# Half-height score pairs, scanned states and a third seven-product batch in a fused retention and Fourier-mix kernel

## The chip, the cores and the metric

The kernel runs on one core of a Trainium2 chip. The metric is the device time of one execution in microseconds; lower is better. Engines are named as in the profile: PE (TensorE, with PEld for its weight loads), DVE (VectorE), ACT (ScalarE), POOL (GpSimd), SP (SyncE, which issues most of the DMAs).

## The reference

Two stages follow each other. The first is a retention recurrence over q, k, v of 4 batches, 8 heads, 768 steps, 64 channels; the second a Fourier mix with a two-layer network on 4 x 768 rows of 512 channels.

```python
gamma = 1.0 - 2.0 ** (-5.0 - np.arange(H))
for t in range(S):
    state = gamma[None, :, None, None] * state + np.einsum('bhd,bhe->bhde', k[:, :, t], v[:, :, t])
    y[:, :, t] = scale * np.einsum('bhd,bhde->bhe', q[:, :, t], state)
...
X = np.fft.fft(np.fft.fft(x, axis=1), axis=2)
u = x + np.real(X)
un = (u - mu) / np.sqrt(var + 1e-06)
out = u + np.maximum(un @ w_ch1, 0.0) @ w_ch2
```

Here x is y with the heads side by side (4 x 768 x 512), w_ch1 is 512 x 2048, w_ch2 2048 x 512.

## The kernel before, in words

**Retention.** The sequence is cut into six chunks of 128 steps. Heads go in pairs: a pair's 2 x 64 channels fill 128 partitions. Within a chunk, scores are keys times queries (`wkA`, in PSUM), multiplied by a causal mask with the head's decay (`atm`, in SBUF), and then multiplied with the values; across chunks, a 64 x 64 state per head is carried (`wkK` in PSUM, `s16` in SBUF) and multiplied with the queries. Both products add up in `wkY`, which ACT scales and writes as x.

The first batch and the other three differ in how they do that. The first batch keeps both heads' queries in one tile of 128 partitions and multiplies each head's 64 partitions apart: `am_unit` (L563) makes twelve matmuls of 64 x 128 with 128 columns, alternating between the two heads, `kv0_unit` (L591) ten of 64 columns for the states, and one DVE scan (`sc_unit`, L600) carries the states of both heads over all chunks with the decay table `gk5`. Batches two to four pad the queries with zeros, so that each head has a full tile of 128 partitions with the other head's half empty (`q16z`, `qTz`, padded by `pad_unit` and `qt_zeros`): `a_unit` (L689) makes six matmuls of 256 columns in three parts, each followed by one DVE multiply with the ready mask table `maskp` (L691); `kv_unit` (L708) makes five of 128 columns that compute both heads' states and the cross terms too, carried chunk by chunk by one ACT copy (L713) and four DVE steps (L715); `y_unit` handles one head (L729, L732). Keys and queries are transposed by PE in batch two (`t_unit`, L655; the keys of its last two pairs by DMA) and by DMA in batches three and four (`td_unit`).

**Fourier mix and network.** The transforms are matmuls with cosine and sine tables after folds on DVE (`fold_s`, `fold_d`, `fold_e`; `s1_unit`, L861; `s2_unit`, L1015). POOL adds x (`add_x_unit`, L1048 and L1050), DVE and ACT normalize, and the rows are transposed (`unT_unit`). The first layer is `h0_unit` and `h_unit` (L1118, L1105) with the ReLU on ACT or DVE, the second `ch_unit` (L1140), which works with 512 columns, and `rows_out` (L1130). That is so in the first two batches. In batches three and four the second layer is computed in three groups of 256 rows with seven block products instead of eight: `hp_unit` is the first layer (L1193), `sum_unit` the sums on DVE (`j`, L1211), `p_unit` the products (`p`, L1242) and `add_unit` the adding and the output (`q`, L1256). The differences of weight blocks that these need are made once on DVE by `wsum_unit` (`w`, L1181) and lie in the memory of the input tiles `wide` and of two used tables.

**Order.** It is written out by hand. `FIRST` is the first batch, `LATER` the rest; each name is a unit (kind, batch, index, and after @ the engine for its ReLU or copy). `held` keeps each engine's instructions in written order, so a unit that waits holds up all behind it on that engine. `ps_g` has five PSUM buffers for attention and transforms, `ps_pm` three for the network. Inputs come in two sets of tiles: seven buffers `inp` and the four of `wide`.

Of the kernel before, what the change touches and what calls it, by code (L numbers as in the profile page):

```python
# [11 lines left out]
AF = mybir.ActivationFunctionType  # L12
ALU = mybir.AluOpType
# [6 lines left out]
P = 128  # L20
B, H, S, D = 4, 8, 768, 64
DM = 512
# [30 lines left out]
i02 U01@v i03 x03 X03 U02@a x04 X04 i10 i13 i11 l10 x05 X05 i12 cq10 c0010 n04 i22 l11 c0011  # L53
c0012 n05 TB Z u04 i21 c0013 u05 U05@a r00 n03 c0000 c0001 l12 l13 ck10 t10 cv10 i23 ck11 pz01
c0002 s100 s101 c0003 cq11 O00 a101 cq12 u03 O01 cv11 i20 U03@a a100 t11 c0020 a102 ck12 U04@v
cv12 c0021 s110 c0022 s111 y100 y101 h015@v t12 pz00 a111 cq13 a110 h013@a lq20 a112 s120 h011@a
s121 h01B@v h012@v ck13 cv13 s130 s131 y110 y111 t13 lk20 lv20 lq21 c0023 a120 a122 h01E@a
h010@a a121 a132 ck20 h018@a a131 y121 y120 O02 pz10 a130 h014@a lk21 lv21 h01C@a h016@a y131
fs10 lq22 lk22 lv22 y130 fs11 fd10 r01 h01D@a fd11 h01A@a tk20 h017@a h019@a c0100 c0101 cq20
h01F@a c0102 c0103 g10 fe10 fe11 f100@v f101@v gr11@v f110@v f111@a tq20 gr13@a cq21 gr10@v O03  # L60
c0110 g112 x11 x10 X11 n11 x12 c0120 X10 n10 X12 n12 c0111 lq23 c0112 c0121 pz11 cv20 gr12@a u11
c0113 O04 u10 ck22 u12 c0122 c0123 U10@v U11@a U12@v tq21 a200 ck21 cv22 O05 x13 tk21 X13 s200
s201 cq22 x14 X14 h107@a h103@a h108@a cv21 x15 h10C@a h10B@a h106@v h102@a a202 lk23 h104@v
a201 h105@a h100@a n14 lv23 cq23 h101@a y200 y201 tk22 h10A@v tq22 h10D@a lq30 X15 h10E@a n13
a210 u13 h10F@a ck23 tk23 a212 s210 s211 a211 cv23 n15 U13@d u14 U14@d w10 r10 c1020 c1000
h109@a a222 a220 c1001 y210 y211 tq23 c1002 s230 s231 a221 w11 c1010 c1011 c1012 u15 U15@d s220
c1003 O10 c1013 s221 c1021 w21 lk30 lv30 lq31 r11 a231 y220 a232 y221 h110@a lk31 lv31 fs20 a230
c1022 O11 c1023 O12 y230 h11E@a fd20 y231 fs21 h11D@a fd21 cq30 h119@a h11A@a g20 ck31 h117@a
h113@a fe21 h11F@a tq30 h112@a h115@a f211@a fe20 ck30 f210@v w20 f200@v gr20@v f201@a h111@v
gr21@v gr23@v lq32 lk32 h11C@a h116@v tk31 tk30 gr22@a g212 lv32 x21 cq31 x20 h114@a X21 h11B@v  # L70
tq31 n21 cv31 c1110 X20 x23 X23 c1120 h118@a x22 cv30 s310 x25 u21 n20 lq33 u20 U21@d X22 c1121
cq32 w41 c1100 n23 n22 cv32 x24 c1111 c1101 c1112 U20@d ck32 c1102 c1103 O13 X24 a301 lk33 a302
u22 c1113 O14 c1122 a312 w40 c1123 U22@d a311 X25 O15 n25 H202@s s300 ck33 s301 H204@s H203@a
u23 a300 s311 H201@a a310 H200@a j20104 H207@a j20178 y300 w31 H205@s y301 w30 tk32 j20204
j20404 cq33 H206@s j20147 j20347 r20 j20378 y310 U23@d tk33 j20278 y311 p201 p204 lv33 cv33 tq32
q201 j20247 j20304 j20447 tq33 p202 q202 p206 p205 q206 p207 u25 n24 q205 u24 j20478 q207 s320
s330 r21 s321 H217@a j21178 a320 p203 q203 j21278 U24@d a322 a321 a331 H213@s H210@s s331 j21478
H212@a H211@a j21104 j21304 j21204 j21378 a332 H215@a H214@s j21404 H216@a a330 y321 j21147
j21347 p211 j21247 q211 j21447 y320 fs30 y331 y330 p214 p216 fs31 q216 fd31 p215 q215 U25@d p217
g30 fd30 fe30 fe31 p212 p213 q212 f300@a f301@a q217 f310@v f311@a q213 H221@a g312 x31 gr30@v  # L80
X31 x30 X30 n31 n30 H226@a H222@s H223@a H220@a j22104 j22204 u31 x32 H224@b H225@s H227@b r22
j22404 p221 q221 j22147 j22178 gr31@a X32 j22247 u30 gr33@a p224 p225 j22278 j22304 p226 p222
U31@d j22447 U30@d j22378 q225 gr32@a j22347 j22478 q226 n32 u32 q222 p223 q223 p227 q227 x33
H300@s x35 H304@a r30 H302@v H303@b H301@a j30104 X33 H306@s H305@s n33 U32@d j30204 j30404
j30304 H307@b j30148 X35 j30248 j30448 x34 p301 q301 p304 p305 p302 q305 p306 j30348 q306 u33
U33@d q302 p303 q303 n35 p307 q307 X34 H317@v n34 H314@a u34 U34@d H312@v H315@a H313@a H311@b
H310@s H316@s j31104 j31204 j31148 j31248 j31348 j31304 r31 j31404 p311 q311 p314 p315 q315
j31448 p312 p316 q316 q312 u35 U35@d p313 q313 p317 q317 H321@a H320@a H322@a j32103 j32303
H327@b H326@a j32168 H324@a H323@s j32203 H325@s j32403 j32368 j32136 j32236 r32 j32436 p321
p322 j32336 p324 p325 q321 j32268 p326 q322 q325 j32468 p323 q326 p327 q323 q327  # L90
# [7 lines left out]
def kernel(  # L98
# [13 lines left out]
    def pool(name, bufs, **kw):  # L112
# [6 lines left out]
    tp = pool("tp", 2)  # L119
    ap_ = pool("ap", 2)  # L120
# [8 lines left out]
    obp = pool("obp", 2)  # L129
# [15 lines left out]
    maskp = const.tile([P, NHP, 2, P], f32, tag="maskp")  # L145
# [3 lines left out]
    gk5 = const.tile([P, 2, D, NCH - 1], f32, tag="gk5")  # L149
    t2 = gk5[:, 0].rearrange("p e c -> p (e c)").bitcast(f16)[:, 0:520].rearrange(  # L150
        "p (n w) -> p n w", n=4)
# [58 lines left out]
    def filler32(n):  # L210
        def run():
            for _ in range(n):
# [7 lines left out]
    turns = early + [x for b in (1, 2) for i in range(4) for x in [(n, b, i) for n in "qkv"]  # L220
                     if x not in early]
# [81 lines left out]
    nc.gpsimd.memset(gk5[:, :, :, 0:1], 0.0)  # L303
# [6 lines left out]
    def gk_unit(i, eng):  # L310
        copy = nc.scalar.copy if eng == "a" else nc.gpsimd.tensor_copy
        hp = ORD0[i]
        return lambda: copy(gk5[:, i % 2, :, 1:], gk2[:, hp:hp + 1].unsqueeze(1).to_broadcast(
            [P, D, NCH - 2]))

    def late_consts():
        with tc.issue_after(lb[0]["una"].ins):
            for h in range(H):
                nc.scalar.activation(maskp[:, h // 2, h % 2], maskf, AF.Copy, bias=0.0,
                                     scale=float(gam[h] ** (-P)))  # L320
# [16 lines left out]

    def pad_unit(j, h):
        return lambda: nc.vector.memset(qzs[j][:, h, :, D - D * h:P - D * h], 0.0)

    def qt_zeros():
        for j in range(2):
            nc.vector.memset(qts[j][0:D, 1], 0.0)
            nc.vector.memset(qts[j][D:P, 0], 0.0)
# [88 lines left out]
    for j in range(2):  # L433
        x = const.tile([P, NCH, 2, XW], f16, tag=f"x16_{j}", name=f"x16_{j}")
        xts.append(x)
        qz = const.tile([P, 2, NCH, P], f16, tag=f"q16z_{j}", name=f"q16z_{j}")
        qzs.append(qz)
        qt = const.tile([P, 2, NCH, P], f16, tag=f"qTz_{j}", name=f"qTz_{j}")
# [16 lines left out]
    def cq_unit(b, i):  # L455
        def run():
            q16, q32 = qzs[i % 2], in_of.pop(("q", b, i))
            if b < NPE:
                q16 = q16_of[b, i] = q16.rearrange("p h c d -> p (h c d)")[
                    :, 0:NCH * P].rearrange("p (c h d) -> p c h d", c=NCH, h=2)  # L460
                nc.gpsimd.tensor_scalar(out=q16, in0=q32.rearrange("p h c d -> p c h d"),
                                        scalar1=1.0, scalar2=1.0, op0=ALU.mult, op1=ALU.mult)
                return
            for h2 in range(2):
                dst = q16[:, h2, :, D * h2:D * h2 + D]
                nc.gpsimd.tensor_scalar(out=dst, in0=q32[:, h2], scalar1=1.0, scalar2=1.0,
                                        op0=ALU.mult, op1=ALU.mult)
            q16_of[b, i] = q16
        return run
# [20 lines left out]
    def q0_unit(i):  # L490
        def run():
            q16 = q16_of[0, i] = qzs[i % 2].rearrange("p h c d -> p (h c d)")[
                :, 0:NCH * P].rearrange("p (c h d) -> p c h d", c=NCH, h=2)
# [34 lines left out]
    def t0_unit(i, part):  # L528
        def run():
            if part == 0:  # L530
                at[0, i] = dict(kT=tp.tile([P, NCH, P], f16, tag="kT", name="kT"),
                                qT=qts[i % 2][:, 0])
# [62 lines left out]
    def sc_unit(i):  # L595
        def run():
            st = at[0, i]
            st["s16"] = sp.tile([P, D, NCH - 1], f16, tag="s16", name="s16",
                                padded_shape=[P, P, NCH - 1])
            nc.vector.tensor_tensor_scan(  # L600
                out=st["s16"].rearrange("p e c -> p (e c)"),
                data0=gk5[:, i % 2].rearrange("p e c -> p (e c)"),
# [41 lines left out]
    def t_unit(b, i):  # L644
        def run():
# [3 lines left out]
            for dst, src in ((qT, q16_of[b, i]), (kT, kd_of[b, i])):  # L649
# [7 lines left out]
                if dst is qT:  # L657
                    for h2 in range(2):
                        rows = slice(D * h2, D * h2 + D)
                        nc.scalar.copy(  # L660
                            qT[rows, h2].rearrange("p c t -> p (c t)").rearrange(
# [771 lines left out]
```

## Time and profile before

| | before |
|---|---|
| median of 3 runs | 237.56 us (237.46 to 237.72) |
| profiled execution | 237.73 us |
| its span in the profile | 235.7 us |
| busy: PE, DVE, ACT, POOL | 223.2, 197.0, 133.3, 83.6 us |
| first matmul of the network | 32.8 us |
| last DVE instruction starts | 231.74 us |
| TensorE clock granted | full in all slices |

Busy times are shares of the span by engine; they overlap. A row of the timeline or of the chain has start, length and work; a row of groups has line, engine, operation, output and inputs, count, busy us, mean ns of one, and the engine's idle time before them.

### The profile page before, as it was taken

To read this page: it belongs to the slowest core of one execution; us is meant where nothing else is said; L and a number is where in the kernel's file an instruction comes from. 1 tells how busy PE (TensorE), PEld (TensorE's weight loads), DVE (VectorE), ACT (ScalarE), POOL (GpSimd) and SP (SyncE) were. 2 spreads that over 40 slices of the span, in tenths; PEclk is the share of its full clock that TensorE was granted. 3 is DMA by queue.
4 is the path that set the end of the run, shared out by engine and by line. 5 is a ranking of instruction groups with operands and counts; after the bars stand their busy time and mean duration, and the time that the engine had idled before them with its cause. 6 is when DMAs were issued, how large, how long until landed. Compare 5 with 4: busy or idle time off the path is not lost.

```text
span 235.7 us, 5892 instructions
## 1 busy us (share of the span) xinstructions
PE 223.2 (95%) x2271; PEld 168.9 (72%) x2271; DVE 197.0 (84%) x490; ACT 133.3 (57%) x304; POOL 83.6 (35%) x148
## 2 busy tenths in 40 slices
PE   0898999999999999999999999999989999999993
PEld 0366769767765747665667548998979899888882
DVE  8789986978898989797998899889998987949373
ACT  5989758486687258554286435834617846062530
POOL 8377902567332078830016992210004221200000
PEclk9999999999999999999999999999999999999999
DMA  7999999999999987997899979784002230121202
GB/s 175 235 268 271 209 207 207 210 236 255 231 228 239 193 189 182 168 199 114 175 222 270 172 148 220 168 127 132 4 0 92 38 116 7 50 86 25 89 21 70
DMA packets 100955, 36.82 MB, mean 156 GB/s; under 512 B 91456, under 2 KB 97984, under 8 KB 100928
## 3 DMA queue, kind: packets, MB, share of 16 engines
q1 hardware_dynamic: 96704, 32.25, 67.7%
q0 software_dynamic: 4224, 4.19, 10.8%
q8 instruction: 18, 0.29, 0.5%
q14 instruction: 9, 0.07, 0.1%
HBM read 27.26 MB, written 6.29 MB: 142 GB/s over the span
## 4 chain that ended last, share of the span: by engine, by line
PE 84%; DVE 5%; SPq 5%; DMA 3%; POOL 1%; issue 1%; ACT 0%; POOLq 0%; DVEq 0%
PE psh L1193 18%; PE psc L1140 18%; PE psh L1105 13%; PE ps L1242 13%; PE psh L1118 5%; SPq L257 5%; PE wkA L689 3%; PE ps L861 3%; DMA wide<-in_q_dram 3%; PE pq L1015 2%; PE wkY L732 1%; PE wkK L708 1%; PE wkY L729 1%; PE ps L842 1%; PE tq L655 1%; DVE xab L758 1%
## 5 line engine op out<-in xcount | busy, mean ns | idle before, releaser
L1098 ACT ACTIVATE ht<-psh 128x384 f16<-128x384 f32 (+2 forms) x106 | 49.0, 480 | 44.4 <-PE psh L1193 28.5
L1140 PE MATMUL psc<-w,ht 128*128 128x512 f16 x192 | 45.8, 379 | 0.0
L1193 PE MATMUL psh<-unT,w 128*128 128x256 f16 x384 | 44.6, 273 | 0.0
L1193 PEld LDWEIGHTS <-w 128*128 128x128 f16 x384 | 37.1, 98 | 4.1
L1048 POOL TENSOR_TENSOR u<-u,x 128x256 f32<-128x256 f32 x21 | 13.3, 635 | 64.2 <-DVE u L1022 53.0
L1105 PE MATMUL psh<-unT,w 128*128 128x384 f16 x192 | 34.8, 326 | 0.0
L1242 PEld LDWEIGHTS <-ht 128*128 128x128 f16 x296 | 27.8, 98 | 3.4 <-ACT ht L1098 0.2
L1140 PEld LDWEIGHTS <-ht 128*128 128x128 f16 x192 | 18.0, 98 | 16.8
L1105 PEld LDWEIGHTS <-w 128*128 128x128 f16 x192 | 18.2, 98 | 10.6 <-issue 0.2
L691 DVE TENSOR_TENSOR atm<-wkA,maskp 128x512 f16<-128x512 f32 x36 | 23.5, 678 | 0.8 <-PE wkA L689 0.5
L477 POOL TENSOR_SCALAR kd<-k,gexp 128x384 f16<-128x384 f32 x20 | 12.2, 624 | 33.1 <-PE psh L1105 22.8
L1211 DVE TENSOR_TENSOR ht<-ht 128x512 f16<-128x512 f16 (+3 forms) x48 | 15.9, 352 | 7.5 <-ACT ht L1098 7.1
L1064 ACT ACTIVATE un<-u,stats 128x512 f16<-128x512 f32 x21 | 15.1, 725 | 11.4 <-issue 7.7
L715 DVE SCALAR_TENSOR_TENSOR s<-s,gk,wkK 128x128 f16<-128x128 f16 x48 | 16.5, 345 | 4.0 <-ACT s L713 2.3
L1095 DVE TENSOR_SCALAR ht<-psh 128x512 f16<-128x512 f32 (+2 forms) x24 | 13.4, 567 | 6.2 <-ACT ht L1098 3.4
L1242 PE MATMUL ps<-wide,ht 128*128 128x256 f16 x144 | 18.5, 273 | 0.0
L739 ACT ACTIVATE x<-wkY,gexp 128x384 f16<-128x384 f32 x24 | 13.0, 584 | 7.3 <-PE wkY L732 7.3
L1059 DVE BATCH_NORM_STATS2 bst<-u 128x6 f32<-128x512 f32 x21 | 14.3, 683 | 0.6 <-POOL u L1050 0.2
L1050 POOL TENSOR_TENSOR u<-u,x 128x256 f32<-128x256 f32 x21 | 13.3, 635 | 0.0
L689 PE MATMUL wkA<-qTz,kT 128*128 128x256 f16 x72 | 12.6, 273 | 0.0
L1242 PE MATMUL ps<-w,ht 128*128 128x256 f16 x96 | 12.4, 273 | 0.0
L1118 PEld LDWEIGHTS <-w 128*128 128x128 f16 x192 | 11.4, 98 | 1.2 <-issue 0.3
(205 smaller groups left out, 415.1 us busy)
## 6 DMA issues: line engine op xcount, KB each, us to landing
out_dram<-ob SPq DMA_DIRECT2D x23, 256.0 KB, 2.3
k<-in_k_dram SPq DMA_DIRECT2D x13, 384.0 KB, 5.3
v<-in_v_dram SPq DMA_DIRECT2D x12, 384.0 KB, 6.0
q<-in_q_dram SPq DMA_DIRECT2D x11, 384.0 KB, 5.3
w<-in_moe_w_ch_dram POOLq DMA_DIRECT2D x8, 512.0 KB, 10.7
wide<-in_q_dram SPq DMA_DIRECT2D x5, 384.0 KB, 6.2
wide<-in_v_dram SPq DMA_DIRECT2D x4, 384.0 KB, 6.1
wide<-in_k_dram SPq DMA_DIRECT2D x3, 384.0 KB, 6.3
```

Of the source, the lines that this page charges most:

```text
L689: nc.tensor.matmul(wk[:, c2], st["kT"][:, c, :], st["qT"][:, :, c, :], start=True, stop=True)
L691: nc.vector.tensor_tensor(out=st["atm"][:, 2 * part:2 * part + 2], in0=wk, in1=maskp[:, PAIR_ORDER[i]].unsqueeze(1).to_broadcast([P, 2, 2, ...
L715: nc.vector.scalar_tensor_tensor(out=s16[:, c], in0=s16[:, c - 1], scalar=gk2[:, hp:hp + 1], in1=wk[:, c - c0], op0=ALU.mult, op1=ALU.add)
L1059: nc.vector.bn_stats(bst, u[:, kb, :])
L1064: nc.scalar.activation(un, u[:, kb, :], AF.Identity, bias=stats[:, kb, 0:1], scale=-1.0)
L1098: nc.scalar.activation(dst, src, AF.Relu, bias=0.0, scale=-1.0)
L1105: nc.tensor.matmul(psh, w116[:, cb, fb * P:(fb + 1) * P], unT[:, cb, rt * 384:(rt + 1) * 384], start=(cb == 0), stop=(cb == 3))
L1118: mm = nc.tensor.matmul(psh[:, f], w116[:, cb, fb * P:(fb + 1) * P], unT[:, cb, kb * P:(kb + 1) * P], start=(cb == 0), stop=(cb == 3))
L1140: nc.tensor.matmul(psc_of[b, rb], ht16[:, fb, rb3 * P:(rb3 + 1) * P], w216[:, fb, :], start=(fb == 0), stop=(fb == NFB - 1))
L1193: nc.tensor.matmul(psh[:, t], w116[:, cb, fb * P:(fb + 1) * P], unT[:, cb, g * 256:(g + 1) * 256], start=(cb == 0), stop=(cb == 3))
L1211: nc.vector.tensor_tensor(out=out_, in0=x, in1=y, op=op)
L1242: nc.tensor.matmul(dst, lhsT, rhs[:, c0:c1], start=(n == 0 and (name is not None or k == 5 and m == 1)), stop=(n == 7), skip_group_check=True)
```

## The change

- **Queries unpadded, scores half-height.** In batches two to four the queries stay two heads to a tile, as in the first batch; `pad_unit`, `qt_zeros`, the padding and the table `maskp` go. `a_unit` makes the scores of three chunks in two PSUM tiles, one for each head, by six matmuls of 64 x 128, two halves a pair. For each head, the mask is applied on DVE in one step, or by ACT (scale) and POOL (select): `@v` both heads on DVE, `@a` both by ACT and POOL, `@b` one each. In the new table 19 of the 48 go to DVE, 29 to ACT and POOL.
- **States by scans.** `kv_unit` makes ten matmuls of 64 columns and one scan on DVE. `gk5` has the decays of all four pairs, so the table of half transforms `t2` gets a tile of its own.
- **Outputs.** `y_unit` handles both heads of a pair at once, with half-height products of query and state.
- **Seven products in batch two, too.** `LATER` has `H`, `j`, `p`, `q` for batch two where it had `h` and `c`, and the weight differences `w` come earlier. `wide` is then taken after the second batch's inputs, and batches three and four load into the seven `inp` buffers alone.
- **Buffers and order.** `tp`, `ap` and `obp` have three buffers instead of two; `LATER` is written anew. The last products are P2 and P3 instead of P3 and P7.

```diff
-i02 U01@v i03 x03 X03 U02@a x04 X04 i10 i13 i11 l10 x05 X05 i12 cq10 c0010 n04 i22 l11 c0011
...
+i02 U01@v x03 X03 U02@a i13 x05 i11 i23 l10 l11 i22 cq10 x04 i20 i10 i21 i03 X05 n03 TB c0020
...
-    tp = pool("tp", 2)
-    ap_ = pool("ap", 2)
+    tp = pool("tp", 3)
+    ap_ = pool("ap", 3)
...
-    obp = pool("obp", 2)
+    obp = pool("obp", 3)
...
-    maskp = const.tile([P, NHP, 2, P], f32, tag="maskp")
...
-    gk5 = const.tile([P, 2, D, NCH - 1], f32, tag="gk5")
+    gk5 = const.tile([P, NHP, D, NCH - 1], f32, tag="gk5")
...
-        n = turns.index((name, b, i)) % 11 if b < 3 else 0
+        n = turns.index((name, b, i)) % 11 if b < 2 else 0
...
-    def a_unit(b, i, part):
+    def a_unit(b, i, half, eng):
...
-            wk = ps_g.tile([P, 2, 2, P], f32, tag="g", name="wkA")
-            for c2 in range(2):
-                c = 2 * part + c2
-                nc.tensor.matmul(wk[:, c2], st["kT"][:, c, :], st["qT"][:, :, c, :],
-                                 start=True, stop=True)
-            nc.vector.tensor_tensor(
-                out=st["atm"][:, 2 * part:2 * part + 2], in0=wk,
-                in1=maskp[:, PAIR_ORDER[i]].unsqueeze(1).to_broadcast([P, 2, 2, P]),
-                op=ALU.mult)
+            wk = [ps_g.tile([P, 3, P], f32, tag="g", name="wkA", padded_shape=[P, 4, P])
+                  for _ in range(2)]
+            for c3 in range(3):
+                c = 3 * half + c3
+                for h2 in range(2):
+                    sl = slice(D * h2, D * h2 + D)
+                    nc.tensor.matmul(wk[h2][:, c3, :], st["kT"][sl, c, :], st["qT"][sl, c, :],
+                                     start=True, stop=True)
+            for h2 in range(2):
+                dst, scale = st["atm"][:, 3 * half:3 * half + 3, h2, :], \
+                    float(gam[2 * PAIR_ORDER[i] + h2] ** (-P))
+                if eng == "v" or eng == "b" and h2 == 1:
+                    nc.vector.scalar_tensor_tensor(
+                        out=dst, in0=wk[h2], scalar=scale,
+                        in1=maskf.unsqueeze(1).to_broadcast([P, 3, P]), op0=ALU.mult, op1=ALU.mult)
+                else:
+                    nc.scalar.activation(dst, wk[h2], AF.Copy, bias=0.0, scale=scale)
+                    nc.gpsimd.affine_select(out=dst, in_=dst, compare_op=ALU.is_ge, fill=0.0,
+                                            base=0, pattern=[[0, 3], [1, P]],
+                                            channel_multiplier=-1)
...
-    def kv_unit(b, i, half):
+    def kv_unit(b, i):
...
-            for c in range(c0, c0 + n):
-                nc.tensor.matmul(wk[:, c - c0, :], kd[:, c].rearrange("p a b -> p (a b)"),
-                                 v16[:, c].rearrange("p a b -> p (a b)"),
-                                 start=True, stop=True)
...
+            for c in range(NCH - 1):
+                for h2 in range(2):
+                    nc.tensor.matmul(wk[64 * h2:64 * h2 + 64, :, c], kd[:, c, h2, :],
+                                     v16[:, c, h2, :], start=True, stop=True)
...
+            nc.vector.tensor_tensor_scan(
+                out=st["s16"].rearrange("p e c -> p (e c)"),
+                data0=gk5[:, ORD0.index(PAIR_ORDER[i])].rearrange("p e c -> p (e c)"),
+                data1=wkf, initial=0.0, op0=ALU.mult, op1=ALU.add)
...
-    def y_unit(b, i, h2):
+    def y_unit(b, i):
...
-                nc.tensor.matmul(yk[:, c, :], qT[:, h2, c, :], s16[:, c - 1, sl],
-                                 start=(c == 1), stop=False, skip_group_check=True)
...
+                for h2 in range(2):
+                    sl = slice(64 * h2, 64 * h2 + 64)
+                    nc.tensor.matmul(yk[h2][:, c, :], qT[sl, c, :], s16[sl, :, c - 1],
+                                     start=(c == 1), stop=False, skip_group_check=True)
```

More of the change, by code (lines that the diff above doesn't have):

```diff
@@ L59 @@
[L59 to L64, printed above, removed]
@@ L219 @@
     early = [(n, 0, i) for n, i in LOADS0] + [("q", 1, 0), ("q", 1, 1)]
[L220 to L221 removed]
+    turns = early + [x for i in range(4) for x in [(n, 1, i) for n in "qkv"] if x not in early]
     def in_tile(name, b, i):
[L224 removed]
+        n = turns.index((name, b, i)) % 11 if b < 2 else 0
         if n >= 7:
@@ L312, in gk_unit, with run @@
         hp = ORD0[i]
[L313 to L320, printed above, removed]
+        def run():
+            if i > 1:
+                nc.gpsimd.memset(gk5[:, i, :, 0:1], 0.0)
+            copy(gk5[:, i, :, 1:], gk2[:, hp:hp + 1].unsqueeze(1).to_broadcast([P, D, NCH - 2]))
+        return run
     def half_tables():
@@ L456, in run @@
         def run():
[L457 to L468, printed above, removed]
+            q16_of[b, i] = qzs[i % 2]
+            nc.gpsimd.tensor_scalar(out=qzs[i % 2], in0=in_of.pop(("q", b, i)).rearrange(
+                "p h c d -> p c h d"), scalar1=1.0, scalar2=1.0, op0=ALU.mult, op1=ALU.mult)
         return run
@@ L657, in run @@
                 if dst is qT:
[L658 to L661, printed above, removed]
-                                "p (t c) -> p t c", c=NCH),
-                            tq[rows].rearrange("p c t -> p t c"))
+                    nc.scalar.copy(qT.rearrange("p c t -> p (c t)").rearrange(
+                        "p (t c) -> p t c", c=NCH), tq.rearrange("p c t -> p t c"))
                 else:
@@ L719, in kv_unit @@
         return run
-    def y_unit(b, i, h2):
+    def y_unit(b, i):
         def run():
             st = at[b, i]
-            h = 2 * PAIR_ORDER[i] + h2
             v16, s16, atm, qT = v16_of[b, i], st["s16"], st["atm"], st["qT"]
-            yk = ps_g.tile([P, NCH, D], f32, tag="g", name="wkY", padded_shape=[P, 8, D])
-            sl = slice(64 * h2, 64 * h2 + 64)
+            yk = [ps_g.tile([P, NCH, D], f32, tag="g", name="wkY", padded_shape=[P, 8, D])
+                  for _ in range(2)]
@@ L728, in run @@
             for c in range(1, NCH):
-                nc.tensor.matmul(yk[:, c, :], qT[:, h2, c, :], s16[:, c - 1, sl],
-                                 start=(c == 1), stop=False, skip_group_check=True)
-            for c in range(NCH):
-                nc.tensor.matmul(yk[:, c, :], atm[:, c, h2, :], v16[:, c, h2, :],
-                                 start=False, stop=(c == NCH - 1), skip_group_check=True)
-            x = xts[b % 2]
-            if h < 4:
-                dst = x[:, :, 0, 64 * h + 1:64 * h + 65]
-            else:
-                dst = x[:, :, 1, 513 - 64 * h:449 - 64 * h:-1]
@@ L1384, in later_unit @@
         n = [int(c, 16) for c in name[len(kind):]]
-        return with_engine[kind](*n, eng or "a") if kind in with_engine else later[kind](*n)
+        return with_engine[kind](*n, eng or ("v" if kind == "a" else "a")) if kind in with_engine else later[kind](*n)
     pin()
```

134 lines of the change are left out of this document (63 added, 71 removed).

## The prediction

> **What bounds the kernel now.** I read the page first: busy time, then the chain of work that ended last.
>
> ```profile
> PE 223.2 (95%) x2271; PEld 168.9 (72%) x2271; DVE 197.0 (84%) x490; ACT 133.3 (57%) x304; POOL 83.6 (35%) x148
> ...
> PE 84%; DVE 5%; SPq 5%; DMA 3%; POOL 1%; issue 1%; ACT 0%; POOLq 0%; DVEq 0%
> ```
>
> PE is busy 95% of the span and holds 84% of the chain. An average says nothing of stages, so next I read stretches of the span: everything between the first batch and the last product, and the one stretch in it where PE stood.
>
> ```profile
> 45.00:225.00 180.00, 179.28 (x1713) 136.16 (x1711) 154.45 (x378) 97.75 (x227) 57.59 (x91) 1.00 0.74 146
> 165.00:180.00 15.00, 14.31 (x178) 12.76 (x176) 14.18 (x37) 6.92 (x16) 0.00 (x0) 1.00 0.08 30
> ```
>
> The columns are the length, then the busy time of PE, PEld, DVE, ACT and POOL, the granted clock, DMA. In 180 us PE is idle for 0.72 us, of which 0.69 lie in 165 to 180. There the chain passes from PE to DVE, through the folds of batch four:
>
> ```profile
> 174.49 0.58 DVE ee L799
> ```
>
> So from 45 us on the kernel is a row of matmuls with one hole. Whatever the change takes from DVE can win back that 0.7 us and no more; the rest of its worth is what it does to the length of the row of matmuls. I price that from start to start, since the ends of matmuls are modelled.
>
> **The score, state and output matmuls.** Batch one already does them in the form that the change gives to the others: half-height score pairs (L563), states of 64 columns (L591), half-height products of query and state (L623). The timeline of PE there has start, length, work:
>
> ```profile
> 18.54 0.69 PE L842 MATMUL ps<-ssp,xab 128*128 128x193 f16 x6
> 19.16 0.51 PE L563 MATMUL wkA<-qTz,kT 64*128 64x128 f16 x12
> 19.60 0.60 PE L842 MATMUL ps<-csp,xab 128*128 128x193 f16 x5
> ...
> 22.64 0.35 PE L613 MATMUL wkY<-v,atm 128*128 128x64 f16 x6
> 22.92 0.52 PE L623 MATMUL wkY<-s,qTz 64*128 64x64 f16 x10
> 23.38 0.69 PE L842 MATMUL ps<-ssp,xab 128*128 128x193 f16 x6
> ...
> 24.32 0.69 PE L842 MATMUL ps<-csp,xab 128*128 128x193 f16 x6
> 24.94 0.47 PE L591 MATMUL wkK<-v,kd 128*64 128x64 f16 x10
> 25.34 0.68 PE L842 MATMUL ps<-ssn,xab 128*128 128x193 f16 x6
> 25.86 0.68 PE L842 MATMUL ps<-csp,xab 128*128 128x193 f16 x6
> ```
>
> Six L842 followed by more of their kind last 0.52 (25.34 to 25.86). Six followed by half-height or half-width work last 0.62: 18.54 to 19.16, and 24.32 to 24.94. Going into another array form costs PE 0.10 us. Twelve scores last 0.44 (19.16 to 19.60); at 128 columns in pairs, six times the 0.056 that the row below shows for one full-height matmul of 128 columns are 0.34, so the way back is 0.10 too, and six scores alone are 0.17. Ten L591 last 0.40 and ten L623 0.46, way back included.
>
> What batches two to four do instead, from the chain (start, length, work):
>
> ```profile
> 51.81 0.28 PE wkK L708 x5
> ...
> 52.95 0.22 PE wkA L689 x2
> ...
> 58.48 0.14 PE wkY L729 x5
> 58.63 0.17 PE wkY L732 x6
> ```
>
> Per pair of heads: three score parts 0.66, states 0.28, outputs twice 0.14 and 0.17 or 0.63 with the second half's 0.15; together 1.57. After: two score halves, each 0.10 in, 0.17, 0.10 back, are 0.74; states 0.10 and 0.40; outputs 0.10, 0.46, and twelve full-height ones at 0.17 for six, 0.35. Together 2.15. Twelve pairs: 12 x 0.58 = +7.0. Where two such units adjoin, a change of form is saved: 96 changes if all stood alone, 81 in the order of the changed kernel, 15 x 0.10 = -1.5. Attention on PE: +5.5. How they stand there, first pair of batch two, before (kd is the decayed key, w_113 the second layer's weights):
>
> ```order
> L708 MATMUL wkK<-v_1085,kd_1064 128x128
> L1140 LDWEIGHTS ht_128
> L1140 MATMUL psc<-w_113,ht_128 128x512
> ...
> L689 LDWEIGHTS kT
> L689 MATMUL wkA<-qTz_201,kT 128x256
> L1118 LDWEIGHTS w_112
> ```
>
> and PE at the same place after the change (L630 are transposes, L1118 is now the second layer):
>
> ```order
> L630 MATMUL tq<-ident_159,kd_1058 128x128
> L663 LDWEIGHTS kT
> L663 MATMUL wkA<-qTz_201,kT 128x128
> ...
> L1118 MATMUL psc<-w_113,ht_128 128x512
> L687 LDWEIGHTS kd_1041
> L687 MATMUL wkK<-v_1067,kd_1041 64x64
> ...
> L663 MATMUL wkA<-qTz_201,kT 128x128
> L1118 LDWEIGHTS ht_128
> ```
>
> Every unit now changes the form on the way in and out; here a state and a score half adjoin and save one.
>
> The Trainium skill, TensorEngine Tiling (Array Packing), Key Properties, says the same against this change: another tiling mode, not merely another tile, drains TensorE. It states no price; by it alone the sign of this term stays open.
>
> **The second batch's second layer.** Rows of the chain for each kind of matmul:
>
> ```profile
> 72.45 2.60 PE psh L1105 x16
> 75.05 1.73 PE psc L1140 x8
> ...
> 192.90 6.11 PE psh L1193 x56
> 199.24 6.11 PE ps L1242 x56
> ```
>
> First layer: 32 units of four L1105 at 0.65 are 20.8; 24 units of eight L1193 at 0.873 are 20.95. Second layer: 24 units of four L1140 at 0.865 are 20.8; three groups of seven products at 0.873 are 18.3. Net -2.3. PE's row of matmuls grows by 5.5 - 2.3 = **+3.2**.
>
> **The other engines.** Groups by line, busy us and mean ns of one:
>
> ```profile
> L691 DVE TENSOR_TENSOR atm<-wkA,maskp 128x512 f16<-128x512 f32 x36 | 23.5, 678 | 0.8 <-PE wkA L689 0.5
> L715 DVE SCALAR_TENSOR_TENSOR s<-s,gk,wkK 128x128 f16<-128x128 f16 x48 | 16.5, 345 | 4.0 <-ACT s L713 2.3
> L577 DVE SCALAR_TENSOR_TENSOR atm<-wkA,maskf 128x384 f16<-128x384 f32 x16 | 8.0, 548 | 1.6 <-PE wkA L563 1.6
> L600 DVE TENSOR_TENSOR_SCAN s<-gk,wkK 128x320 f16<-128x320 f32 x4 | 3.3, 816 | 0.3 <-POOL gk L313 0.2
> L739 ACT ACTIVATE x<-wkY,gexp 128x384 f16<-128x384 f32 x24 | 13.0, 584 | 7.3 <-PE wkY L732 7.3
> ```
>
> DVE loses 23.5 and 16.5; it gets 19 masks at 0.548 (10.4) and 12 scans at 0.816 (9.8). A third seven-product batch brings half of what two batches spend now on sums (L1211) and on adding (L1256):
>
> ```profile
> 0.00:236.00 236.00, 20.91 (x64) 1.00 0.79 156
> 0.00:236.00 236.00, 20.09 (x38) 1.00 0.79 156
> ```
>
> that is 20.5, less the six row outputs that go. DVE ends some 3 us lighter, and its work in batches three and four, where the hole is, falls by more. I take the hole as gone: -0.7. The other 29 mask halves cost ACT 29 x 0.584 = 17 us and POOL a select each. The one select in the trace is a third as wide:
>
> ```profile
> 2.55 0.29 POOL L299 TENSOR_SCALAR_AFFINE_SELECT maskf<-maskf 128x128 f32<-128x128 f32 x1
> ```
>
> so 0.29 to 0.88, and I take 0.6, twice the row for three times the columns. ACT near 60% and POOL near 43% stay off the bound; what counts is lateness, a rival below. The unpadded queries halve what eight transposing DMAs move; no PE time depends on it while the hole is the only one. The mask table's eight ACT copies and the padding's memsets go, and two small memsets come to POOL in batch one: beside a full PE, 0.
>
> One new wait I can price. Batch two's first keys come late, and the transposes of its second pair now stand sooner:
>
> ```profile
> 44.27 2.24 SPq L242 DMA_DIRECT2D k<-in_k_dram  x1
> ...
> 51.29 1.14 POOL L477 TENSOR_SCALAR kd<-k,gexp 128x384 f16<-128x384 f32 x2 [0.98 <-DMA k<-in_k_dram]
> ...
> 49.38 0.67 PE tq L655 x12
> ...
> 54.50 0.67 PE tq L655 x12
> ```
>
> The first pair's transposes have about the same PE work ahead of them as before (two units of the first layer more; two of the second and one set of transposes less), so they start near 49.4 again. Then only eight L1140 (1.73) precede the second pair's, where 4.5 us stood. Their key half would come near 52.0; POOL delivers at 52.4, held by the landing of that key. +0.5. For waits of its kind that I cannot see I add another 0.5, less than the hole that goes.
>
> The end: the last product was P7, with one add of 512 columns behind it; now it is P3 in two halves, the last add 128 wide.
>
> ```profile
> 230.87 0.35 DVE L1256 SCALAR_TENSOR_TENSOR ob<-ps7e,stats,u 128x128 f32<-128x128 f32 x1
> 231.74 0.75 DVE L1256 SCALAR_TENSOR_TENSOR ob<-ps,stats,u 128x512 f32<-128x512 f32 x1 [0.52 <-PE ps L1242]
> ```
>
> That is -0.4 at best; SP has one more output to issue behind adds that end close together, so between -0.4 and +0.3: -0.2.
>
> **Sum.** The profiled execution took 237.73, 0.17 over the median of the runs. 237.73 + 3.2 - 0.7 + 0.5 + 0.5 - 0.2 = 241.0, or **240.9** as a median.
>
> **Rivals.** (a) Faster: changes of form cost nothing in a full row of matmuls, the drain being covered by queued weight loads. Then a pair takes 0.34 + 0.30 + 0.71 = 1.35 instead of 1.57, 12 x 0.22 = -2.6, with -2.3 and the other terms' +0.1 makes 232.9, 232.8 as a median. It decides from the price: 81 changes at 0.059 us break even, the rows say 0.10, alike at two places with PE full on both sides. 0.10, and 0.06 for a price so near 0.06 that the result falls at or a little under the time before.
> The Trainium skill, TensorE: Matmul & The Clock Gate, Part 3, models packed tiles as the length of one matmul plus about 4 ns a tile and charges nothing for entering or leaving; by that rule, rival (a) holds, and the rows of batch one speak against it.
>
> (b) Slower still: masks come late. A half that goes by ACT and POOL needs 2 x 0.584, then 2 x 0.6, about 2.5 us with a matmul's tail, and the PE work between the last such half of a pair and its outputs is 2.5 to 3.5 us. That covers it unless POOL stands at a cast whose load has not landed. Loads do hold it up:
>
> ```profile
> 154.12 1.03 POOL L486 TENSOR_SCALAR v<-v 128x768 f16<-128x768 f32 x1 [5.51 <-DMA v<-in_v_dram]
> ```
>
> On POOL, late in batch two, stood casts alone (q16z, kd, v16 are the casts of query, key, value):
>
> ```order
> L486 TENSOR_SCALAR v_1211<-wide 128x768
> L461 TENSOR_SCALAR q16z_205<-wide 128x768
> L477 TENSOR_SCALAR kd_1331<-k_1060,gexp 128x6x64 x2
> L486 TENSOR_SCALAR v_1334<-v_1062 128x768
> L477 TENSOR_SCALAR kd_1426<-k_1386,gexp 128x6x64 x2
> ```
>
> and now:
>
> ```order
> L463 TENSOR_SCALAR v_1359<-v_1233 128x768
> L674 AFFINE_SELECT atm<-atm 128x3x128 x2
> L444 TENSOR_SCALAR q16z_200<-q_1314 128x768
> L674 AFFINE_SELECT atm<-atm 128x3x128 x2
> L454 TENSOR_SCALAR kd_1440<-k_1329,gexp 128x6x64 x2
> ```
>
> The cast of batch three's first query stands ahead of masks that batch two's last pair waits for. Masks 1 to 3 us late there and at one or two later pairs, and the hole kept, give 2 to 6 us more: 244.5, from the point where that load lands over 1 us after the masks are ready to be cut. 0.20.
>
> (c) The change does not do what it says: half-height scores run one after the other, at 0.056 instead of 0.028 each. 144 x 0.028 = +4.0, 244.9. The twelve in 0.44 speak against it. 0.02.
>
> (d) DVE's relief is worth more than the hole: it cannot be, with 0.72 us of idle PE in 180.
>
> **How the numbers follow.** Forecast 0.62, (a) 0.16 with its near case, (b) 0.20, (c) 0.02. 0.2% is 0.5 us, about what a measurement of this kernel can tell from no change. Faster by more than that takes (a): 0.11. Within it: a price of form changes near 0.06, or of 0.08 with the hole and every new wait gone: 0.05. Slower: 0.84. The range: the unknown costs give +3.2 - 0.7 + 0 - 0.4 = 2.1 at the low end, and less by 1.6 if the price of a change is 0.08, so 238.1; at the high end most of (b), 244.5. That leaves out (a) and the last of (b), under 2 in 10.
>
> **What would show it.** Right: PE at 9 tenths in every slice as before, L663, L687 and L705 showing the 0.10 us gaps at both ends in batches two to four, L691 and L715 gone from DVE, DVE under 80%, the chain still on PE. Each step: any full-height line followed by L663 starting 0.10 late; the second pair's key transposes held by POOL near 52 us; no DVE stretch in the chain of batch four; the last add 128 wide. Wrong: no gap where the form changes and a last matmul before 228 us (a); PE waiting in the outputs (L705, L711) for POOL's selects (b).

## The result, and the profile after

The changed kernel takes 239.96 us (median of 4 runs, 239.57 to 240.44) against 237.64 us (4 runs, 237.46 to 237.87) for the kernel before beside it: a ratio of 1.0098, 95% interval 1.0077 to 1.012. It is slower, by 2.3 us (1%) where 3.3 were forecast. The profiled execution took 240.10 us, its span is 238.3 us.

The page of after, busy time and the chain by engine:

```profile
PE 225.8 (95%) x2539; PEld 177.5 (74%) x2539; DVE 188.4 (79%) x448; ACT 140.2 (59%) x321; POOL 98.4 (41%) x171
...
PE 84%; DMA 6%; DVE 3%; POOL 2%; ACT 2%; SPq 1%; issue 1%; POOLq 0%; ACTq 0%
```

The same stretches as before (length, then busy time of PE, PEld, DVE, ACT, POOL, the clock, DMA):

```profile
45.00:225.00 180.00, 179.37 (x1926) 141.00 (x1925) 143.95 (x332) 105.75 (x250) 71.34 (x111) 1.00 0.66 137
165.00:180.00 15.00, 15.00 (x172) 13.38 (x171) 12.53 (x30) 7.80 (x19) 0.00 (x0) 1.00 0.14 37
```

PE is as full as it was: 0.63 us idle in 180, instead of 0.72. The hole in 165 to 180 is gone, DVE has 10.5 us less to do over the 180 us, and still the program is longer. So PE has more to do. PE's timeline shows where; first states, scores and second-layer products of batch two, then outputs:

```profile
54.86 0.47 PE L687 MATMUL wkK<-v,kd 128*64 128x64 f16 x10
55.27 0.34 PE L663 MATMUL wkA<-qTz,kT 64*128 64x128 f16 x6
55.54 1.04 PE L1118 MATMUL psc<-w,ht 128*128 128x512 f16 x4
56.51 0.34 PE L663 MATMUL wkA<-qTz,kT 64*128 64x128 f16 x6
...
60.93 0.53 PE L705 MATMUL wkY<-s,qTz 64*128 64x64 f16 x10
61.39 0.52 PE L711 MATMUL wkY<-v,atm 128*128 128x64 f16 x12
61.84 0.53 PE L705 MATMUL wkY<-s,qTz 64*128 64x64 f16 x10
```

Four L1118 ahead of scores last 0.97 (55.54 to 56.51), where four at 0.216 (eight took 1.73 before) make 0.865: 0.10 goes at the entry. Six scores last 0.27 until the next full-height matmul may start, 0.17 of it work.

The one wait of PE left behind the first batch that is longer than 0.04 us, by the list of PE's waits (total, times, longest):

```profile
PE tq L630 <- POOL kd L454: 0.6, 1, 0.6
```

and what holds it, in the chain:

```profile
44.41 6.55 DMA k<-in_k_dram
...
51.12 1.16 POOL kd L454 x2
52.27 0.05 issue
52.32 0.51 PE tq L630 x6
```

The new work off PE, by groups:

```profile
L674 POOL TENSOR_SCALAR_AFFINE_SELECT atm<-atm 128x384 f16<-128x384 f16 x29 | 15.4, 554 | 29.3 <-ACT atm L673 29.3
L673 ACT ACTIVATE atm<-wkA 128x384 f16<-128x384 f32 x29 | 12.8, 491 | 8.5 <-PE wkA L663 8.4
L669 DVE SCALAR_TENSOR_TENSOR atm<-wkA,maskf 128x384 f16<-128x384 f32 x19 | 9.8, 549 | 6.0 <-PE wkA L663 5.9
```

And the last add, with the two kinds of output DMA (count, KB, us to landing):

```profile
234.85 0.35 DVE L1234 SCALAR_TENSOR_TENSOR ob<-ps7e,stats,u 128x128 f32<-128x128 f32 x1
```

```profile
out_dram<-ob SPq DMA_DIRECT2D x23, 256.0 KB, 2.4
...
out_dram<-ob SPq DMA_DIRECT2D x2, 64.0 KB, 1.7
```

### The profile page after: what moved, and what is told of

It reads as the page before. It is cut to its first block, busy times and chain, and to the rows that moved or that the text cites. A ratio compares the mean times of both kernels' runs of the same rounds, so it can differ in the third digit from the quotient of the medians.

```text
span 238.3 us, 6421 instructions
## 1 busy us (share of the span) xinstructions
PE 225.8 (95%) x2539; PEld 177.5 (74%) x2539; DVE 188.4 (79%) x448; ACT 140.2 (59%) x321; POOL 98.4 (41%) x171
## 4 chain that ended last, share of the span: by engine, by line
PE 84%; DMA 6%; DVE 3%; POOL 2%; ACT 2%; SPq 1%; issue 1%; POOLq 0%; ACTq 0%
PE psh L1171 27%; PE ps L1220 23%; PE psc L1118 7%; PE psh L1083 5%; DMA v<-in_v_dram 3%; DMA k<-in_k_dram 3%; PE ps L839 3%; PE wkA L663 3%; PE wkY L711 2%; PE wkY L705 2%; PE psh L1096 2%; PE wkK L687 2%; PE pq L993 2%; PE ps L820 1%; PE pq L905 1%; SPq L253 1%
## 5 line engine op out<-in xcount | busy, mean ns | idle before, releaser
L1076 ACT ACTIVATE ht<-psh 128x256 f16<-128x256 f32 (+2 forms) x108 | 48.1, 469 | 47.8 <-PE psh L1171 34.7
L1171 PE MATMUL psh<-unT,w 128*128 128x256 f16 x576 | 66.2, 273 | 0.0
L1171 PEld LDWEIGHTS <-w 128*128 128x128 f16 x576 | 55.5, 98 | 6.8 <-DMA unT<-un 0.3
L1189 DVE TENSOR_TENSOR ht<-ht 128x512 f16<-128x512 f16 (+2 forms) x57 | 22.3, 411 | 8.2 <-ACT ht L1076 7.6
L674 POOL TENSOR_SCALAR_AFFINE_SELECT atm<-atm 128x384 f16<-128x384 f16 x29 | 15.4, 554 | 29.3 <-ACT atm L673 29.3
L1118 PE MATMUL psc<-w,ht 128*128 128x512 f16 x96 | 23.2, 379 | 0.0
L673 ACT ACTIVATE atm<-wkA 128x384 f16<-128x384 f32 x29 | 12.8, 491 | 8.5 <-PE wkA L663 8.4
L1234 DVE SCALAR_TENSOR_TENSOR u<-ps,stats,u 128x256 f32<-128x256 f32 (+2 forms) x27 | 14.9, 563 | 2.1 <-PE ps L1220 1.8
L1234 DVE SCALAR_TENSOR_TENSOR ob<-ps,stats,u 128x256 f32<-128x256 f32 (+2 forms) x27 | 14.8, 561 | 1.6 <-PE ps L1220 0.9
L1118 PEld LDWEIGHTS <-ht 128*128 128x128 f16 x96 | 8.6, 98 | 8.4
L669 DVE SCALAR_TENSOR_TENSOR atm<-wkA,maskf 128x384 f16<-128x384 f32 x19 | 9.8, 549 | 6.0 <-PE wkA L663 5.9
```

The costliest lines, as they stand in the source:

```text
L674: nc.gpsimd.affine_select(out=dst, in_=dst, compare_op=ALU.is_ge, fill=0.0, base=0, pattern=[[0, 3], [1, P]], channel_multiplier=-1)
L1076: nc.scalar.activation(dst, src, AF.Relu, bias=0.0, scale=-1.0)
L1118: nc.tensor.matmul(psc_of[b, rb], ht16[:, fb, rb3 * P:(rb3 + 1) * P], w216[:, fb, :], start=(fb == 0), stop=(fb == NFB - 1))
L1171: nc.tensor.matmul(psh[:, t], w116[:, cb, fb * P:(fb + 1) * P], unT[:, cb, g * 256:(g + 1) * 256], start=(cb == 0), stop=(cb == 3))
L1189: nc.vector.tensor_tensor(out=out_, in0=x, in1=y, op=op)
L1234: nc.vector.scalar_tensor_tensor(out=out_, in0=in_, scalar=r, in1=u_, op0=ALU.mult, op1=ALU.add)
```

## The experiments

A form is the height and width of the array that a matmul uses: full (128 x 128), half height (64 x 128) or half width (128 x 64). The theory: a change of the array's form costs PE about 0.10 us each way, whatever stands around it, and attention loses by that what the seven products win. The rivals: changes are free in a full row and the loss lies in the half-size matmuls, in the masks by way of ACT and POOL, or in the new order.

### The price alone: price_half, price_full, price_cols

To the kernel *before*, two small matmuls ahead of each of the 48 first-layer units of batches three and four; three versions that differ in the form of these two (in price_cols, not shown, they are the two halves of the columns, 128 x 64 each).

```diff
             psh = ps_pm.tile([P, 2, 256], f32, tag="pm", name="psh")
+            for z in range(2):
+                rows = slice(0, 64)          # price_full: all 128 partitions
+                nc.tensor.matmul(psh[:, z, 0:64], w116[rows, 0, n * P:(n + 1) * P],
+                                 unT[rows, 0, g * 256:g * 256 + 64], start=True, stop=True)
```

> The kernel before, with two matmuls of 64 x 128 by 64 columns (half height, both in the upper half of the array) ahead of each of the 48 first-layer units of batches three and four, where PE is full; the first-layer sum that follows overwrites them. Theory (a change of form costs about 0.095 us in and 0.11 us back): 48 x (0.095 + 0.036 + 0.146) = +13 us, about 251. Rival (changes of form are covered by queued weight loads; the after's extra time lies in the half-size matmuls themselves): 48 x 2 x 0.036 = +3.5 us, about 241.

> The same 96 extra matmuls of 64 columns at the same places, at full height: no change of form. Both theories: 96 x 0.029 = +2.8 us, about 240.4. What tells them apart is the difference to the half-height version: 10 us by the theory (96 changes of form at 0.10), under 1 us by the rival.

> The same again with full height and half width (128 x 64, the two halves of the columns side by side, as the states have it). Theory: a change of form costs the same whichever side is halved, 0.09 in and 0.10 back: 48 x (0.093 + 0.04 + 0.15) = +13 us less what of the two matmuls overlaps, 250 to 251. Rival: the drain belongs to half height alone, +1.5 to +2.8, about 240.

Measured: 250.25 us at half height (ratio 1.0531, 1.0505 to 1.0557), 240.22 at full height (1.011, 1.0085 to 1.0135), 249.92 at half width (1.0515, 1.0489 to 1.0541). Between the first two lie 10.0 us for 96 changes: 0.104 each, with 0.5 us in it because the second small matmuls start later (39 ns behind the first instead of 28) and 0.5 because the first full-height matmul behind them takes 119 ns instead of 110. PE's timeline, half height:

```profile
144.17 1.05 PE L1197 MATMUL psh<-unT,w 128*128 128x256 f16 x8
145.15 0.23 PE L1192 MATMUL psh<-unT,w 64*128 64x64 f16 x2
145.31 1.05 PE L1197 MATMUL psh<-unT,w 128*128 128x256 f16 x8
```

full height:

```profile
143.85 1.04 PE L1196 MATMUL psh<-unT,w 128*128 128x256 f16 x8
144.72 0.22 PE L1191 MATMUL psh<-unT,w 128*128 128x64 f16 x2
144.78 1.04 PE L1196 MATMUL psh<-unT,w 128*128 128x256 f16 x8
```

Eight matmuls of 256 columns last 0.87 ahead of full-height work and 0.98 ahead of half-height work; the small pair lasts 0.06 or 0.16. From start to start, the last full-height matmul takes 205 ns instead of 109 (+96), the last half-height one 123 instead of 29 (+94). The way in costs 93 to 97 at all 48 places, behind matmuls of 64 to 256 columns alike. At half width the way in is 93, and the pair and its way back take 152 together. Rival "free in a full row" is dead, and with it rival (a) of the prediction.

The traces also show why queued weight loads do not cover a change. At full height the load of a small matmul's weights starts 27 to 108 ns ahead of the matmul, while the one before it still runs. At every change, in price_half and at all 81 in batches two to four of the changed kernel, it starts 1 to 5 ns ahead: no load was started before the change. What the array does in the 0.095 us before that, the traces do not show.

By the Trainium skill, TensorEngine Tiling (Array Packing), Key Properties, a change of mode drains TensorE: the runs agree, as nothing starts for some 0.095 us, and give the price that it doesn't. By the Trainium skill, TensorE: Matmul & The Clock Gate, Part 3, a packed stretch lasts one matmul's length and about 4 ns a tile more, with nothing for the way in and out: inside a stretch the runs agree (starts 3 ns apart in a pair), but the rule misses 0.19 us around each.

### The second batch's seven products: no_seven2, seven_only

In the changed kernel, batch two's `p`, `j` and `q` give way to plain products of the same `H`:

```diff
-... p104 ... p101 q101 ... p105 j10404 j10304 ... p106 ...
+... C1000 ... C1001 ... C1002 ... C1003 O10 ...
```

> The changed kernel with batch two's second layer by eight blocks of 512 columns a row block (48 x 4 matmuls at 0.216) in place of its three groups of seven products; its first layer and all else stay. DVE loses that batch's sums and adds. Theory (seven products are worth 3 x (6.92 - 6.11) = 2.4 us of PE, and DVE isn't the bound): 239.96 + 2.4 = 242.4. Rival (what they add to DVE costs as much as they save on PE): 240.

242.29 us (ratio 1.0213, 1.0193 to 1.0232), 2.3 more than the changed kernel by the medians, 2.7 by the ratios. From start to start, the second layer of batches two to four takes 58.5 us of PE (21.3 in the 96 plain products of 512 columns, 37.2 in sevens) instead of 56.3: +2.2. The term is confirmed, and what the products add to DVE is hidden. The profiled execution of this run, 243.32 us, was the longest of its four; 0.9 us of its distance are the late key of batch two, ahead of the edited part:

```profile
PE tq L625 <- POOL kd L449: 1.5, 2, 1.1
```

The other way round, the old attention in the new order:

```diff
-    (units s, a, y of the change)        a110@v a111@v
+    (units s, a, y of before)            a110 a111 a112
```

> The changed kernel's order, loads and seven products in batch two, with the old attention (padded queries, scores of 256 columns at full height, masks and states on DVE). Theory (the seven products take 2.3 us from PE, the changes of form in attention cost some 5): 237.6 - 2.3 - 0.4 at the end, with the hole in batch four kept or a little larger, 235 to 236. Rival (changes of form cost nothing and the new order or the seven products' sums on DVE are what made the changed kernel slower): 239 to 240.

255.66 us (1.0758, 1.0721 to 1.0796): a miss, and not for a reason of either theory. 45 to 225 us of it:

```profile
45.00:225.00 180.00, 166.09 (x1669) 133.75 (x1667) 156.96 (x372) 92.53 (x219) 59.13 (x91) 0.99 0.70 139
```

PE is idle for 13.9 us of 180. All masks and states are on DVE, in an order written for a lighter DVE, and PE waits for them, and for what stands behind them on DVE and ACT, at many places. So this run says nothing of the price of the seven products; it says that order and load go together, as the next one shows in a cleaner way.

### The masks: masks_dve

```diff
-t11 a101@b r00 c0003 c0012 s10 a100@b c0021 a110@v ...
+t11 a101@v r00 c0003 c0012 s10 a100@v c0021 a110@v ...
```

(all 48 mask halves `@v`)

> The changed kernel, with all 48 mask halves on DVE (29 x 0.55 = 16 us more there; ACT loses 13 and POOL 15). Theory (PE is the bound, the masks by ACT and POOL were never waited for): 239.9, at most 0.5 either way. Rival (masks that come late by ACT and POOL are part of the loss): 238 or less; the other side of it, if DVE then is the bound in places as it was before: 240.5 to 242.

244.19 us (1.0282, 1.0255 to 1.0309), 4.2 more than the changed kernel. That is above what either theory had. The same stretch, and the largest waits of PE that the changed kernel has shorter or not at all:

```profile
45.00:225.00 180.00, 175.39 (x1877) 136.76 (x1876) 154.63 (x356) 92.43 (x216) 57.16 (x82) 1.00 0.69 136
```

```profile
PE tq L630 <- POOL kd L454: 1.3, 2, 1.1
PE ps L839 <- DVE stats L1054: 1.1, 1, 1.1
PE wkY L705 <- DVE s L690: 0.6, 1, 0.6
```

DVE has 154.6 us of work there, within 0.2 of the kernel before, and PE stands idle for 4.6 us instead of 0.7. This profile is that of the longest of six executions (243.15 to 245.58 us), and 0.7 of the 4.6 us are more of the late key, which the masks do not touch; the rest are new waits. So the masks by way of ACT and POOL are not part of the loss; in this order, without them, the change would cost 4 us more.

### The late key: t11_later

```diff
-t11 a101@b r00 c0003 c0012 s10 a100@b
+a101@b r00 c0003 c0012 t11 s10 a100@b
```

> The changed kernel, with the transposes of batch two's second pair moved behind one more score half and eight second-layer matmuls (1.7 us of PE work later). Theory: the 0.69 us of idle PE at 51.5 us goes, 239.96 - 0.6 = 239.3. Rival: something else is late next (the key's cast, the state's scan), and the wait only moves: 239.9.

239.18 us (1.0079, 1.0049 to 1.0109). Its stretch from 45 to 225 us:

```profile
45.00:225.00 180.00, 179.96 (x1936) 141.98 (x1934) 143.91 (x332) 106.21 (x252) 71.06 (x111) 1.00 0.65 138
```

0.04 us of idle PE are left. Against the changed kernel that is 0.8 us by the medians and 0.5 by the ratios, whose intervals overlap; but the trace shows the wait itself gone, and nothing in its place. Of the runs below, pad_y, pad_adj and flat_state build on this version, y_full and sy_full on the changed kernel itself.

### Full-height outputs: y_full, sy_full, pad_y, pad_adj

The first try wrote the scanned states into zeroed 128 x 128 blocks, `sblk`, by two scans of 64 partitions:

```diff
+            st["s16"] = sblk[i % 2]
+            for h2 in range(2): (scan of partitions 64 * h2 ... into st["s16"][sl, h2])
-                    nc.tensor.matmul(yk[h2][:, c, :], qT[sl, c, :], s16[sl, :, c - 1],
+                    nc.tensor.matmul(yk[h2][:, c, :], qT[:, c, :], s16[:, h2, :, c - 1],
```

> The changed kernel, with the products of query and state at full height: the scans write each head's state into its own corner of a zeroed 128 x 128 block, in two scans of 64 partitions, and ten matmuls of 128 x 128 by 64 columns take the place of the half-height pairs. Theory: per pair of heads 0.095 in, 0.33 and 0.146 become 0.29: 12 x 0.28 = -3.3, about 236.7. Rival (changes of form free): 12 x 10 x (0.036 - 0.029) = -0.9, about 239, and the twelve added scans (10 us more on DVE) may give that back.

> The same, and the states at full height, too: ten matmuls of 128 x 128 by 64 columns into two PSUM tiles, of which each scan reads its half. Theory: against the changed kernel -3.3 - 12 x 0.11 and two more changes of 0.09, about 235.2. Rival: as the version with full-height outputs alone, about 239; a tenth buffer conflict in PSUM could cost 1.

249.6 and 249.96 us (1.052 both), where 236.7 and 235.2 were expected: misses, and no clean test of the theory. The blocks go by a pair's number, but batch three takes its fourth pair ahead of its third. So the fourth pair's scans fill the block that the second pair's outputs have yet to read: these outputs wait for the scans, and the second pair's queries are multiplied with the fourth pair's state. PE's waits for scans, in y_full:

```profile
PE wkY L711 <- DVE sblk L697: 3.3, 3, 2.3
```

Two things stand beside it in the traces. Behind the wait of 2.3 us the granted clock falls: 0.66 over 110 to 115 us (0.52 over 109 to 116 in sy_full, behind a wait of 2.1). The page of y_full has it in one of 40 slices:

```profile
PEclk9999999999999999997999999999999999999999
```

And the full-height products take 0.074 us each, start to start: 9.4 us in all, waits between them included, against 5.5 for the half-height pairs. So its products are slower than the pairs that they replace, which the next run shows without the mix-up.

pad_y does it without DVE: queries padded again, the scanned state as it is, and `tp`, `ap` and `obp` with two buffers again.

```diff
-                    nc.tensor.matmul(yk[h2][:, c, :], qT[sl, c, :], s16[sl, :, c - 1],
+                    nc.tensor.matmul(yk[h2][:, c, :], qT[:, h2, c, :], s16[:, :, c - 1],
```

> The changed kernel with t11 later, and with padded queries as before, so that the products of query and state run at full height against the dense scanned state (ten of 128 x 128 by 64 columns a pair of heads); scores stay half-height, masks, scans and the order as they are, so that DVE has the same work. 60 form changes in batches two to four instead of 81. Theory: per pair of heads 0.095 + 0.48 becomes 0.29, 12 x 0.28 = -3.3 from 239.2: about 236. Rival (form changes cost nothing in the kernel itself): 239.2 - 12 x 10 x 0.007 = 238.4 or more.

245.01 us (1.0322, 1.0308 to 1.0336), 5.8 above t11_later where -3 was expected. The timeline shows why; L727 is the line of the products:

```profile
61.81 0.89 PE L727 MATMUL wkY<-s,qTz 128*128 128x64 f16 x10
62.53 0.53 PE L733 MATMUL wkY<-v,atm 128*128 128x64 f16 x12
62.90 0.90 PE L727 MATMUL wkY<-s,qTz 128*128 128x64 f16 x10
```

Ten of them last 0.72, 0.073 each. In the kernel before, the same shape at full height took 0.14 for five, 0.029 each (the row of the chain at 58.48). What differs is the state's layout, which flat_state below tests alone: a scan leaves the five chunks of a channel side by side, so a chunk's 64 columns lie ten bytes apart. From start to start the 120 matmuls take 8.6 us, where the half-height pairs took 5.5 and their twelve entries 1.1. Much of the rest are new waits, where two half copies on ACT for the padded queries hold up `kT` and two buffers of `ob` instead of three the first layer:

```profile
PE wkA L686 <- ACT kT L658: 1.5, 2, 1.1
PE psh L1105 <- DVE ob L1130: 1.1, 1, 1.1
```

pad_adj puts score halves and states of a pair side by side:

```diff
-s12 cv13 h01B@v w20 a121@b lv20 h013@a a120@b s13
+cv13 h01B@v w20 s12 a121@b lv20 a120@b h013@a ... s13 a131@a a130@v
```

> The same, with the score halves and the states of a pair put side by side where nothing else has to stand between them: 40 form changes instead of 60, the same matmuls. Theory: 20 x 0.10 = -2.0, about 234, if the PSUM buffers that two score halves and a state take at once hold nothing up; with such waits up to +1. Rival (form changes free): no gain, only the waits.

246.17 us (1.0368, 1.0354 to 1.0382): 20 form changes fewer and 1.2 us more. Scores now wait for what empties PSUM; that it comes from five buffers being taken at once is argued, not tested:

```profile
PE wkA L686 <- ACT atm L696: 1.2, 2, 0.6
PE wkA L686 <- DVE u L1025: 0.9, 1, 0.9
```

What the saved changes are worth can't be read from it.

### The state's layout: flat_state

```diff
+            st["flat"] = sp.tile([P, NCH - 1, D], f16, tag="flat", name="flat")
+            nc.vector.tensor_copy(st["flat"], st["s16"].rearrange("p e c -> p c e"))
-                    nc.tensor.matmul(yk[h2][:, c, :], qT[sl, c, :], s16[sl, :, c - 1],
+                    nc.tensor.matmul(yk[h2][:, c, :], qT[sl, c, :], st["flat"][sl, c - 1, :],
```

> The changed kernel with t11 later, and one DVE copy of 320 elements behind each of the twelve scans, which lays the state out with a chunk's 64 columns side by side; the half-height products of query and state read that instead of columns ten bytes apart. The version with padded queries showed 0.073 us for such a matmul at full height, where the kernel before, with columns side by side, takes 0.029. Theory (the pair is slow, 0.073 us, for its strided columns and not for its form): 12 x 5 x 0.044 = -2.6, 239.2 - 2.6 = 236.6, less what 4 us more of DVE work costs. Rival (half-height pairs of 64 columns take 0.073 whatever the layout): 239.2 or a little more.

236.92 us (12 runs; ratio to before 0.9971, 0.9955 to 0.9987). It beats both kernels: 0.3% under before (a small gain, but the interval leaves out 1), and 3.0 us under the changed kernel. The timeline, and the copies:

```profile
60.41 0.32 PE L707 MATMUL wkY<-flat,qTz 64*128 64x64 f16 x10
60.66 0.52 PE L713 MATMUL wkY<-v,atm 128*128 128x64 f16 x12
61.12 0.32 PE L707 MATMUL wkY<-flat,qTz 64*128 64x64 f16 x10
```

```profile
L695 DVE COPY flat<-s 128x320 f16<-128x320 f16 x12 | 6.2, 515 | 0.4
```

Ten half-height products last 0.25 instead of 0.46; a pair follows the one ahead by 0.029 instead of 0.073. Over 120 that is 5.5 us down to 3.0, and the medians fell by 2.3. The 6.2 us that DVE gets are hidden, as the stretch from 45 us on shows:

```profile
45.00:225.00 180.00, 179.95 (x1958) 142.62 (x1956) 151.37 (x351) 106.30 (x254) 70.56 (x111) 1.00 0.67 137
```

## Why the prediction was right, and where its sizes were off

- **Bound.** Right: PE at 95%, the chain 84% on it as before.
- **Attention on PE, +5.5.** Start to start over the trace, the attention matmuls of batches two to four take 19.1 us before and 21.1 after, and the 34 full-height matmuls ahead of them 3.2 more than their own length: +5.2. The price (0.096 and 0.094) was read well from batch one. One part had the right size for the wrong cause: ten L705 at 0.46, way back included, I took as what the form costs; 5 x 0.044 = 0.22 of it is the column spacing, which batch one has as well. Over twelve pairs that is about half of the 5.2: flat_state took 2.5 us of it away and left the forms as they are.
- **Seven products, -2.3.** The second layer took 2.2 less on PE, 2.3 to 2.7 in the times. That run keeps the first layer of the change, whose matmuls take 0.2 more than before (21.0 for 20.8; the prediction had 20.95), so the term is -2.0.
- **The hole, -0.7.** Gone, as said. But "whatever the change takes from DVE can win back that 0.7 us and no more" was true of the order before only: with DVE loaded as before, the new order has 4.6 us of holes (masks_dve, 1.3 of them at the late key). The relief was not a gain but the condition for the rest.
- **The late key, +0.5.** 0.6 by the list of waits, 0.5 to 0.8 when taken away; the key was held by its load's landing, on POOL, as said.
- **Waits of its kind, +0.5.** Not there: 0.63 us of idle PE in all, nearly all of it that key. This term and the next are most of what the sum was too high by.
- **The end, -0.2.** From the start of the last matmul to the end of the span 3.68 us instead of 4.31: -0.6. The last output is issued 0.80 after the start of that matmul instead of 1.09: the shorter add gave its 0.4 (0.75 to 0.35), and SP's two issues in a row took some back, as I had set against it. What I had not counted: the last output is 64 KB instead of 256, and landed 1.67 after its issue instead of 2.00.
- **Select.** 0.554 us, estimated 0.6; scaling on ACT 0.491 for 0.584.
- **Rivals.** (a) and (c) fell by the price and by six scores in 0.17. (b): in the whole trace the list of waits has none of PE for a select; masks were ready.

The sum with these sizes: 5.2 - 2.0 - 0.7 + 0.6 - 0.6 = +2.5; the profiled executions differ by 2.4, their spans by 2.5.

## What to carry to other kernels

Packing two half-height matmuls saves half of their columns and costs 0.19 us a visit (a stretch in the other form, way in and way back). At 0.42 ns a column (0.216 us for 512) it should pay only where a visit has more than some 450 columns to save; that is an estimate from these two figures, and no run tried it. So gather such work before packing it. Price a layout with the reader's side of it: a scan that is cheap on DVE can hand PE columns that it reads at less than half speed, and one copy on an engine with room may win that back. When a change lightens one engine and fills another with new steps, its order has no meaning at the old load; test the parts in an order of their own.

## What the runs showed of the hardware

- A change between full and half height cost PE 0.093 to 0.097 us each way (price_half), the way into half width 0.093 (price_cols). The next weights' load started 1 to 5 ns ahead of its matmul there, instead of 27 to 108.
- The way back cost more where the last columns were spaced: from the last half-height product of query and state to the next full-height matmul 0.181 us, against 0.123 with the state side by side (changed kernel and flat_state).
- 64 f16 columns ten bytes apart took 0.073 us as the moving operand, at full height and in half-height pairs; side by side 0.029. By the Trainium skill, Advanced Engine Details and Errata, Memory Cachelines, two hits on each 16-byte line are needed for full speed. Ten bytes apart give 1.6 a line, an estimate from that figure, and the runs agree.
- The half-width pairs of the states start 3 ns apart, but the next pair starts 0.056 us after the one ahead, hardly sooner than behind two full-width matmuls of 64 columns (0.058). Whether that is their strided PSUM output or their weight loads was not tried.
